# Attention scores: a stage of nine blocks for each head pair from the sixth on, in one tile of four PSUM banks; the last weight pieces fetched behind the first rows of the last stage

## The chip, the cores and the metric

The kernel runs on one core of one Trainium2 chip. The metric is the device time of one execution in microseconds (us); lower is better. [...]

## What is computed

The reference is a windowed causal attention whose output goes through a gated feed-forward network (FFN), all in fp32:

```python
B, H, S, D = 8, 8, 576, 64                     # q, k, v: (B, H, S, D)
scores = q @ k.T / sqrt(D)                     # for each batch and head
rel = pos[:, None] - pos[None, :]
bias = slopes[h] * -abs(rel)
scores = where((rel >= 0) & (rel < 128), scores + bias, -1e9)
attn = softmax(scores) @ v
x = attn.transpose(0, 2, 1, 3).reshape(B * S, H * D)      # 4608 x 512
gate = 1 / (1 + exp(-(x @ w_gate)));  val = x @ w_val     # 512 x 1536
out = (gate * val) @ w_out                                 # 1536 x 512
```

## The kernel before

Work is first put into a graph: every operation is added with an engine, an assumed cost and the keys that it reads and writes. A planner (`Graph.order`) then plays the engines forward and fixes one order of instructions for each engine, which the chip runs in that order; the table `TUNE` shifts the wishes (`want`) of some operations at random and so only changes this order. On the chip each engine runs its own list strictly in order, with semaphores between engines. Transfers are issued by SyncE (SP), accumulating ones by GpSimd (POOL).

**Attention.** A unit is one batch and one pair of heads: 32 units, each with 9 blocks of 128 query rows (the 1152 tokens of two heads). A block's scores come from matmuls on quarter arrays (64 rows by 64 columns; there are four of them, here called lanes, a row half `r` by a column half `h`). A block takes one matmul per column half, each over three 64-key squares (two for the first block of a unit). `scores` (L566) does a *stage*: four blocks until the fifth unit's end (48 blocks in twelve stages), then eight blocks (thirty stages), in banks mm2 to mm5; the blocks run on from unit to unit, so that a stage of eight straddles units. Even blocks go to one row half, odd ones to the other. Then VectorE (DVE) folds each bank in place with a `copy_predicated` (L583, two blocks an instruction), takes scale, bias and row maximum (L591), ScalarE (ACT) takes the exponential and its sum (L595), DVE or ACT normalise (L673, L674), TensorE transposes three blocks at a time (L680), and the weighted sum of values follows: `values` (L718) for the first eight units, `split_values` (L637) from the ninth on. `split_values` has two phases, which stand directly before and directly behind a later stage of scores, all on quarter arrays.

**First FFN pass.** Between stages TensorE works on `ffn` (L808): groups of three 512-column matmuls. It starts as soon as the first weights are decoded and the first four units are through; early on it is short of input.

**Second FFN pass and last stage.** `ffn2` (L998) does the rest of the gated products by a scheme with 7 products per 2 by 2 block; `last` (L1166) does the output projection in three rounds with 15 products each in the sequence 11, 2, 13, 0, 12, 3, 5, 4, 9, 6, 10, 7, 1, 8, 14. Each product reads rows from DRAM (`rows_...`), which are split into a high and a low part (`duo`, L308 and L1147 on ACT, L317 and L1148 on DVE), some after sums and differences (L1086). Its weights were stashed in DRAM and come back by `fetch_o`: the six pieces `wo<-sums_o`, which ACT (L933) and DVE (L934) split after landing, and four pieces `wo_ar0`, `wo_ar5`, `wo_w2s`, `wo_h` (`parts_o`), which need no splitting and are used by the later products only. The meeting of `ffn2` and `last` is called the seam here.

## Time and profile before

| | us |
|---|---|
| median of 3 runs (943.48 to 945.67) | 943.83 |
| the profiled execution, its time | 943.45 |
| the profiled execution, its span | 941.7 |
| TensorE busy in the span | 931.8 (99%) |
| VectorE busy | 788.7 (84%) |
| ScalarE busy | 518.4 (55%) |

The span runs from the first to the last instruction; the time has 1.75 us more, which lie around it. A matmul's end is modelled and matmuls overlap, so a busy TensorE may still wait inside; the chain of work that ended last tells such waits better than the busy time. It is 95% matmuls: L998 45%, L1166 25%, L808 12%, the scores L566 5%, L637 4%, L680 4%.

### The profile page before, as it was taken

The page shows a single profiled execution, that of the slowest core. Times are in us where ns is not written, and L with a number is a line of the kernel's source. Part 1 is how long each engine was busy: PE and PEld are TensorE (multiplying, and loading weights), DVE is VectorE, ACT ScalarE, POOL GpSimd, SP SyncE. Part 2 cuts the span into 40 slices and gives each one's busy share as a digit, 9 for nine tenths or more (in the row PEclk, how much of TensorE's full clock was granted, in tenths as well). Part 3 has the DMA queues.
Part 4 walks back from the last instruction along what each step waited for, and adds up shares of the span by engine and source line. Part 5 has one row for each costly group of instructions (what it writes and reads, how often), then busy time and mean ns, then how long its engine had stood idle before and what let it go on. Part 6 is the DMA issues. An engine that isn't in the chain of part 4 may idle for free.

```text
span 941.7 us, 18317 instructions
## 1 busy us (share of the span) xinstructions
PE 931.8 (99%) x6334; PEld 789.1 (84%) x6334; DVE 788.7 (84%) x1946; ACT 518.4 (55%) x1345; POOL 202.4 (21%) x381
## 2 busy tenths in 40 slices
PE   8999999999999999999999999999999999999998
PEld 6778888888878888888889999988887888888886
DVE  8999888998898996878787697764797899797897
ACT  8998789889874453444344344443563434334341
POOL 3544436545620000112111222211110000000000
PEclk9999999999999999999999999999999999999999
DMA  8887779976937444669878979979897481564441
GB/s 303 282 291 264 234 271 288 345 254 201 330 94 246 145 149 142 146 154 240 234 203 216 295 218 315 249 180 261 251 285 277 156 294 64 167 222 148 121 147 68
DMA packets 91485, 205.94 MB, mean 219 GB/s; under 512 B 9984, under 2 KB 28416, under 8 KB 91008
## 3 DMA queue, kind: packets, MB, share of 16 engines
q1 hardware_dynamic: 79584, 185.56, 57.4%
q0 software_dynamic: 11520, 18.88, 13.4%
q8 instruction: 50, 0.82, 0.3%
q14 instruction: 43, 0.35, 0.1%
q10 hardware_dynamic: 288, 0.33, 0.1%
HBM read 123.73 MB, written 81.00 MB: 217 GB/s over the span
## 4 chain that ended last, share of the span: by engine, by line
PE 95%; ACT 2%; DMA 2%; DVE 1%; issue 0%; SPq 0%; DVEq 0%; ACTq 0%
PE mm L998 45%; PE mm L1166 25%; PE mm L808 12%; PE mm L566 5%; PE mm L637 4%; PE mm L680 4%; DMA rows_ar<-hid 1%; PE mm L718 1%; ACT pb L595 1%; DMA early_ar<-in_q_dram 0%; DVE pb L673 0%; DVE mm L583 0%; ACT kept L595 0%; ACT early_h L308 0%; PE mm L396 0%
## 5 line engine op out<-in xcount | busy, mean ns | idle before, releaser
L998 PE MATMUL mm<-xc,w2s 128*128 128x512 f32 (+1 forms) x2016 | 423.0, 371 | 0.0
L998 PEld LDWEIGHTS mm<-xc,w2s 128*128 128x128 f32 x2016 | 368.7, 188 | 53.3 <-ACT shared L308 0.4
L1166 PE MATMUL mm<-duo,wo 128*128 128x512 f32 x756 | 173.4, 389 | 1.8 <-DVE duo L317 1.8
L1166 PEld LDWEIGHTS mm<-duo,wo 128*128 128x128 f32 x756 | 141.7, 188 | 32.0 <-DVE duo L317 2.6
L808 PE MATMUL mm<-first,first 128*128 128x512 f32 x480 | 130.0, 407 | 0.6 <-ACT early_h L308 0.4
L308 ACT COPY low<-mm 128x512 f32<-128x512 f32 (+1 forms) x93 | 51.3, 553 | 100.6 <-DVE mm L1005 56.4
L808 PEld LDWEIGHTS mm<-first,first 128*128 128x128 f32 x480 | 84.4, 189 | 16.4 <-ACT early_h L308 0.6
L1010 ACT ACTIVATE sg<-mm 128x512 f32<-128x512 f32 (+3 forms) x108 | 54.3, 522 | 71.2 <-PE mm L998 47.6
L1005 DVE TENSOR_TENSOR mm<-mm,low 128x512 f32<-128x512 f32 (+1 forms) x96 | 62.1, 651 | 36.4 <-PE mm L998 34.6
L756 POOL DMA_DIRECT2D hidq<-later_hs x47 | 42.2, 970 | 205.7 <-DVE later_hs L1015 133.8
L595 ACT ACTIVATE pb<-pb,st 128x128 f32<-128x128 f32 x216 | 84.4, 398 | 0.9 <-DVE st L591 0.9
L691 POOL TENSOR_SCALAR_AFFINE_SELECT pt<-early_h 128x384 f32<-128x384 f32 x96 | 53.5, 581 | 39.2 <-ACT early_h L308 34.0
L691 POOL TENSOR_SCALAR_AFFINE_SELECT pt<-spread 128x384 f32<-128x384 f32 x96 | 49.5, 544 | 49.0 <-ACT spread L308 45.0
L583 DVE COPY_PREDICATED mm<-early_h,mm 128x256 f32<-128x256 int32 (+1 forms) x144 | 50.6, 389 | 3.3 <-PE mm L566 2.8
L637 PEld LDWEIGHTS mm<-pt,vr 64*64 64x64 f32 x1056 | 42.8, 133 | 9.8 <-ACT pb L595 2.9
L591 DVE CUSTOM_DVE_ANT_0 pb<-mm,early_h 128x128 f32<-128x128 f32 x216 | 49.8, 283 | 0.0
L637 PE MATMUL mm<-pt,vr 64*64 64x192 f32 (+2 forms) x1056 | 46.7, 284 | 0.0
L756 POOL DMA_DIRECT2D hidq<-shared x25 | 22.3, 990 | 101.1 <-DVE shared L1015 91.9
L308 ACT CAST duo<-rows_xr 128x1024 fp32r<-128x1024 f32 x20 | 21.1, 1054 | 39.8 <-PE mm L1166 33.1
L595 ACT ACTIVATION_READ_ACCUMULATOR pb<-pb,st 128x1 f32 x216 | 42.1, 195 | 0.0
L673 DVE TENSOR_SCALAR pb<-pb,st 128x128 f32<-128x128 f32 x164 | 40.2, 292 | 1.8
L308 ACT COPY early_h<-mm 128x384 f32<-128x384 f32 (+3 forms) x76 | 32.4, 446 | 9.9 <-PE mm L637 7.2
(200 smaller groups left out, 1431.8 us busy)
## 6 DMA issues: line engine op xcount, KB each, us to landing
hid<-later_hs SPq DMA_DIRECT2D x38, 256.0 KB, 4.4
vr<-in_v_dram SPq DMA_DIRECT2D x32, 288.0 KB, 5.7
hidq<-later_hs POOLq DMA_DIRECT2D x36, 256.0 KB, 6.0
wraw<-in_moe_w_gate_dram SPq DMA_DIRECT2D x14, 512.0 KB, 5.8
wraw<-in_moe_w_val_dram SPq DMA_DIRECT2D x14, 512.0 KB, 4.4
kr<-in_k_dram SPq DMA_DIRECT2D x11, 576.0 KB, 5.2
wraw<-in_moe_w_out_dram SPq DMA_DIRECT2D x12, 512.0 KB, 7.4
early_h<-in_k_dram SPq DMA_DIRECT2D x10, 576.0 KB, 5.0
```

The source lines that it names most:

```text
L308: g.add("ACT", act_cost(n, psum), lambda: nc.scalar.copy(out(), src()), reads, writes, want, release=release, slack=slack, gives=gives, wa ...
L583: g.add("DVE", dve_cost((a1 - a0) * P, psum=True), lambda b=b, a0=a0, a1=a1: nc.vector.copy_predicated(quads(b)[:, a0:a1, 1:3], before[:, ...
L591: g.add("DVE", 0.21, lambda: nc.vector.tensor_tensor_reduce(pb()[:, e], sp[b][:, a, D:D + P], relm[u.p][:, w], op0=ALU.add, op1=ALU.min, s ...
L595: g.add("ACT", 0.39, lambda: nc.scalar.activation(pb()[:, e], pb()[:, e], AF.Exp, bias=st()[:, e:e + 1], scale=-1.0, accum_out=st()[:, 3 + ...
L637: nc.tensor.matmul(mm[both[h].at][e * D:(e + 1) * D, a - e * S - cuts[h]:b - e * S - cuts[h]], vraw(u)[r * D:r * D + D, c], seen, start=fi ...
L691: nc.gpsimd.affine_select(pt(u)[:, f0:f0 + 2 * n - 1:2, :], both(), [[0, n], step], cmp, 0.0, base=0, channel_multiplier=mult)
L756: g.add("POOL", 1.2, lambda to=to, of=of: nc.gpsimd.dma_start(to(), of(), accum_op=ALU.add), keys, parts_, F, size=2 * kb / 300.0, port=False)
L808: nc.tensor.matmul(mm[s.at][:, 0:wd], w.tile(kind, wi, i)[:, c * P:(c + 1) * P], xpart(x, c)[:, 0:wd], start=(k == 0 and c == 0), stop=(k ...
L998: nc.tensor.matmul(mm[b][:, 0:N2], w.tile2(i, wp)[:, wk, c * P:(c + 1) * P], combo(k, xp, N2)[:, c], start=(start and c == 0 and j == 0), ...
L1005: g.add("DVE", dve_cost(N2, psum=True), lambda: nc.vector.tensor_tensor(o(), bk(b)(), a(), op=ALU.add), [("mm", b), *reads] if okeys else ...
L1010: g.add("ACT", act_cost(y - x, psum=True), lambda x=x, y=y, s=s: nc.scalar.activation(sg[h]()[:, x:y], bk(b)()[:, x:y], AF.Tanh, scale=0.5 ...
L1166: nc.tensor.matmul(mm[b], wo2(z, part_)[:, i, j * P:(j + 1) * P], duo(xp)[:, m], start=start and q == 0 and m == 0 and e == 0, stop=q == 1 ...
```

## The change

From the sixth unit on (`SOON = 5`) a stage is one unit: nine blocks, one `scores` call for each, 27 stages. The five units before it keep stages of four, the last of them five: eleven stages in place of twelve. The nine blocks lie in one tile of four banks (`area`) that is allocated in place of the banks mm2 to mm5 and given back before the second FFN pass (`four_banks`). In it a block begins three squares behind the one before, so that the two column halves of neighbouring blocks share the squares; blocks 0 to 3 and two thirds of block 4 use one row half and banks 0 and 1, the others the other row half and banks 2 and 3. A matmul that would cross a bank is cut in two: 22 matmuls a unit in place of 18. Keys are laid out accordingly, and a unit's key load has 12 of 18 squares (384 KB in place of 576 KB). The fold is four `copy_predicated` a unit, on 64 partitions each and over three or four blocks, all of them ahead of the first maximum. `split_values` of a unit goes around the scores two units later. In `last` the four `parts_o` transfers of the first round depend, in the planner, on the last sum into the rows called "01". The table `TUNE` is another.

```diff
-RUN = 8
-VLATE = RUN
+RUN = 4
 SOON = 5
+MID = NBLK // 2
+KEY1 = 2 * MID - 2
+KEYS = TOK // D - KEY1
...
-    mm = [ps_m.tile([P, NB], F32, name=f"mm{i}") for i in range(8)]
+    mm = [ps_m.tile([P, NB], F32, name=f"mm{i}") for i in range(2)]
+    mm += [None] * 4 + [ps_m.tile([P, NB], F32, name=f"mm{i}") for i in (6, 7)]
+    four = [ExitStack(), None]
+
+    def four_banks(name):
+        four[0].close()
+        four[0] = ctx.enter_context(ExitStack())
+        pool = four[0].enter_context(tc.tile_pool(name=f"ps_{name}", bufs=1, space=PSUM))
+        if name == "area":
+            four[1] = pool.tile([P, 4 * NB], F32, name=name)
+            nc.vector.memset(squares()[0:D, 3], 0.0)
+            nc.vector.memset(squares()[D:P, 3 * MID + 2], 0.0)
+        else:
+            mm[2:6] = [pool.tile([P, NB], F32, name=f"{name}{i}") for i in range(2, 6)]
...
+    def places(i):
+
+        got = []
+        for h in range(2):
+            a, key, step, n = (3 * i + 2, 2 * i, -1, 3) if h == 0 else (3 * i + 1, 2 * i - 1, 1, 3)
+            if (i, h) in ((0, 0), (MID, 1)):
+                a, key, n = 3 * i + 2 + h, 2 * i + h, 1
+            elif (i, h) == (0, 1):
+                a, key, n = a + 1, key + 1, 2
+            elif (i, h) == (MID + 1, 0):
+                n = 2
+            while n:
+                m = min(n, 8 - a % 8)
+                got.append((a // 16, h, a, key, step, m))
+                a, key, n = a + m, key + step * m, n - m
+        return got
+
+    def scores(u, pend=None):
...
+        todo = sorted(x for lane in lanes.values() for x in lane)
+
+        def matmuls():
+            for _, r, h, i, a, key, step, n in todo:
+                rows, k = slice(r * D, r * D + D), key - r * KEY1
+                last = k + step * n
+                keys = kraw(u)[rows, k:(last if last >= 0 else None):step]
+                nc.tensor.matmul(squares()[h * D:(h + 1) * D, a:a + n], qraw(u)[rows, i - r * MID, h * D:(h + 1) * D], keys, start=True, stop=True)
...
+        def fold(h, k0, k1):
+            n, rows, own, off = k1 - k0, slice(h * D, (h + 1) * D), 2 + h, 4 if h == 0 else 1
+            at = lambda x: squares()[rows, 3 * k0 + x:3 * (k1 - 1) + x + 1:3]
+            g.add("DVE", dve_cost(n * D, psum=True), lambda: nc.vector.copy_predicated(
+                at(own), before[rows, 0:1, h].to_broadcast([D, n, D]), at(off)), ["before"],
...
+        for h, k0, k1 in ((0, 1, MID + 1), (1, 1, MID), (0, MID + 2, NBLK), (1, MID + 1, NBLK)):
+            fold(h, k0, k1)
...
-    def fetch_o(z):
-        F, keys = FIRST + 1.5, [("stash_o", z, i) for i in range(14)]
+    def fetch_o(z, after=()):
+        F, keys = FIRST + 1.5, [("stash_o", z, i) for i in range(14)] + list(after)
...
-        for z in range(len(SLOTS), len(SLOTS) + len(LATER)) if t == 0 else ():
-            fetch_o(z)
+        if t == 0:
+            g.add("PY", 0.0, lambda: None, [("row", *rows["01"][1])], ["first rows"], F)
+            for z in range(len(SLOTS), len(SLOTS) + len(LATER)):
+                fetch_o(z, ["first rows"])
```

Three places of the order follow. The first is TensorE at one stage of scores that stands between the two phases of `split_values`. Before, a stage of eight blocks, its sixteen matmuls in banks mm_73 and mm_75, then mm_74 and mm_76, the last phase behind it (mm_72 and mm_77 are the banks of the values):

```order
L566 MATMUL mm_73<-kr_193,qr_200 64x192
L566 MATMUL mm_75<-kr_193,qr_200 64x192
...
L566 MATMUL mm_75<-early_h_181,early_xr 64x128
L566 MATMUL mm_73<-kr_193,qr_200 64x192
L566 MATMUL mm_75<-early_h_181,early_xr 64x128
L566 MATMUL mm_74<-early_h_181,early_xr 64x192
L566 MATMUL mm_76<-early_h_181,early_xr 64x192
...
L637 MATMUL mm_77<-pt_484,vr_242 64x192 x2
L637 MATMUL mm_72<-pt_484,vr_242 64x192 x2
```

Now, the middle and the end of a stage of nine blocks (L646 is the scores' line of the changed kernel, L705 that of the values):

```order
L646 MATMUL area<-early_h_184,early_xr 64x192 x4
L646 MATMUL area<-early_h_184,early_xr 64x64
L646 MATMUL area<-early_h_184,early_xr 64x128
L646 MATMUL area<-early_h_184,early_xr 64x64
L646 MATMUL area<-early_h_184,early_xr 64x128
L646 MATMUL area<-early_h_184,early_xr 64x192
L646 MATMUL area<-early_h_184,early_xr 64x128
L646 MATMUL area<-early_h_184,early_xr 64x192
L646 MATMUL area<-early_h_184,early_xr 64x64
L646 MATMUL area<-early_h_184,early_xr 64x192 x2
L705 MATMUL mm_73<-pt_303,vr_213 64x192 x2
```

A stage now holds one unit and has short matmuls of one and two squares between the long ones; the phases of the values around it are what they were.

The second place is SP's queue at the seam. Before (rows_hs_7410 and the first rows_ar are the two halves of the rows called "12", wo_7390 is the sixth piece of the first six weights):

```order
L313 DMA rows_hs_7348<-hid_128 128x1024
L313 DMA wo_7390<-sums_o_116 128x1792
L313 DMA hid_123<-shared 128x512
L313 DMA wo_ar_7406<-parts_o_120 128x2048
L313 DMA rows_hs_7410<-hid_139 128x1024
L313 DMA wo_ar_7426<-parts_o_119 128x2048
L313 DMA hid_129<-shared 128x512
L313 DMA rows_ar_7456<-hid_140 128x1024
L313 DMA rows_ar_7456<-hidq_169 128x1024
L313 DMA wo_w2s_7469<-parts_o_117 128x3584
```

Now (rows_hs_7495 stands for rows_hs_7410, wo_7500 for wo_7390):

```order
L309 DMA rows_hs_7434<-hid_131 128x1024
L309 DMA hid_126<-shared 128x512
L309 DMA rows_hs_7495<-hid_142 128x1024
L309 DMA wo_7500<-sums_o_119 128x1792
L309 DMA hid_132<-shared 128x512
L309 DMA hid_139<-later_hs_7259 128x512
L309 DMA rows_ar_7570<-hid_143 128x1024
L309 DMA rows_ar_7570<-hidq_172 128x1024
L309 DMA wo_w2s_7668<-parts_o_120 128x3584
L309 DMA wo_h_7671<-parts_o_121 128x1536
L309 DMA rows_wraw_6758<-hidq_173 128x1024
L309 DMA wo_ar_7681<-parts_o_122 128x2048
```

Both wo_ar have moved behind the rows, and the sixth piece wo_7500 has moved from ahead of the rows_hs load to behind it.

The third place is VectorE at the seam. Before (duo_7285 and duo_7381 are the two halves of product 13's rows, then of product 12's):

```order
L934 TENSOR_TENSOR wo_7390<-wo_7390,wo_7461 128x1792
L317 TENSOR_TENSOR duo_7285<-rows_xr,duo_7285 128x1024
L1086 TENSOR_TENSOR rows_tt<-rows_tt,rows_hs_7410 128x1024
L317 TENSOR_TENSOR duo_7381<-rows_xr,duo_7381 128x1024
L1086 TENSOR_TENSOR rows_xr<-rows_tt,rows_xr 128x1024
L317 TENSOR_TENSOR duo_7444<-rows_hs_7348,duo_7444 128x1024
L1086 TENSOR_TENSOR rows_xr<-rows_xr 128x1024
L1086 TENSOR_TENSOR rows_hs_7348<-rows_hs_7348,rows_ar_7456 128x1024
L1086 TENSOR_TENSOR rows_xr<-rows_hs_7348,rows_xr 128x1024
L317 TENSOR_TENSOR duo_7285<-rows_wraw_6619,duo_7285 128x1024
```

Now (duo_7485 and duo_7542 are these halves):

```order
L313 TENSOR_TENSOR duo_7485<-rows_xr,duo_7485 128x1024
L1002 TENSOR_TENSOR wo_7500<-wo_7500,wo_7595 128x1792
L313 TENSOR_TENSOR duo_7542<-rows_xr,duo_7542 128x1024
L313 TENSOR_TENSOR duo_7523<-rows_tt,duo_7523 128x1024
L1154 TENSOR_TENSOR rows_tt<-rows_tt,rows_hs_7495 128x1024
L313 TENSOR_TENSOR duo_7531<-rows_hs_7434,duo_7531 128x1024
L1154 TENSOR_TENSOR rows_xr<-rows_tt,rows_xr 128x1024
L1154 TENSOR_TENSOR rows_hs_7434<-rows_hs_7434,rows_ar_7570 128x1024
L313 TENSOR_TENSOR duo_7485<-rows_wraw_6758,duo_7485 128x1024
```

The splits that product 13 needs no longer stand behind a row sum, but the second of them stands directly behind the split of the sixth weight piece. In both kernels the sum that waits for rows_ar stands ahead of the split for product 12.

## Rows read from the trace of the kernel before

**Rows 1.** The page, busy us (share of the span) xinstructions

```profile
PE 931.8 (99%) x6334; PEld 789.1 (84%) x6334; DVE 788.7 (84%) x1946; ACT 518.4 (55%) x1345; POOL 202.4 (21%) x381
```

**Rows 2.** Busy time by stretch: PE, PEld, DVE, ACT, POOL, clock, DMA share, GB/s

```profile
20.00:40.00 20.00, 19.06 (x238) 14.28 (x238) 19.81 (x104) 18.93 (x76) 10.08 (x25) 1.00 0.77 253
60.00:80.00 20.00, 20.00 (x211) 16.11 (x210) 19.63 (x95) 17.77 (x67) 9.52 (x23) 1.00 0.81 274
```

**Rows 3.** The chain that ended last, 118 to 133 us: start, length, what

```profile
120.08 0.85 PE mm L637 x18
...
120.99 1.30 PE mm L566 x30
122.29 0.66 PE mm L637 x20
...
124.12 0.65 PE mm L680 x6
124.78 3.45 PE mm L808 x15
```

**Rows 4.** The same chain over the whole span

```profile
21.80 1.45 PE mm L566 x30
...
84.09 0.85 PE mm L637 x18
...
142.84 1.46 PE mm L566 x31
...
272.83 413.94 PE mm L998 x1980
...
693.58 3.87 PE mm L1166 x17
```

**Rows 5.** VectorE's groups by form: count | busy us, mean ns | idle before

```profile
L591 DVE CUSTOM_DVE_ANT_0 pb<-mm,early_h 128x128 f32<-128x128 f32 x216 | 49.8, 283 | 0.0
...
L583 DVE COPY_PREDICATED mm<-early_h,mm 128x256 f32<-128x256 int32 x112 | 43.8, 419 | 3.3 <-PE mm L566 2.8
L673 DVE TENSOR_SCALAR pb<-pb,st 128x128 f32<-128x128 f32 x164 | 40.2, 292 | 1.8
...
L591 DVE DVE_READ_ACCUMULATOR2_ANT st<- 128x1 f32 x288 | 23.4, 81 | 0.0
...
L317 DVE TENSOR_TENSOR first<-early_xr,first 128x512 fp32r<-128x512 f32 x16 | 10.3, 682 | 0.0
...
L583 DVE COPY_PREDICATED mm<-early_h,mm 128x128 f32<-128x128 int32 x32 | 9.1, 285 | 0.0
```

**Rows 6.** Timeline of TensorE at the seam: start, length, idle before in brackets

```profile
703.71 7.09 PE L1166 MATMUL mm<-duo,wo 128*128 128x512 f32 x30 [0.16 <-DVE duo L317]
712.43 3.94 PE L1166 MATMUL mm<-duo,wo 128*128 128x512 f32 x16 [1.63 <-DVE duo L317]
```

**Rows 7.** Timeline of SP's queue at the seam

```profile
685.22 0.32 SPq L313 DMA_DIRECT2D wo<-sums_o  x1
...
695.71 0.32 SPq L313 DMA_DIRECT2D rows_hs<-hid  x1
696.08 1.42 SPq L313 DMA_DIRECT2D wo_ar<-parts_o  x1
```

**Rows 8.** Timeline of VectorE at the seam

```profile
696.36 2.03 DVE L934 TENSOR_TENSOR wo<-wo,wo 128x1792 fp32r<-128x1792 f32 x1 [0.22 <-ACT wo L933]
...
711.16 2.35 DVE L317 TENSOR_TENSOR duo<-rows_wraw,duo 128x1024 fp32r<-128x1024 f32 x2
```

**Rows 9.** ScalarE's groups, 680 to 712 us

```profile
L933 ACT CAST wo<-wo 128x1792 fp32r<-128x1792 f32 x3 | 5.2, 1718 | 0.0
```

**Rows 10.** Landing of wo (560 to 700); accumulating transfers, 300 to 400 and 660 to 690

```profile
DMA to landing us min/median/max: 5.0/7.0/7.9
...
hidq<-later_hs POOLq DMA_DIRECT2D x3, 256.0 KB, 4.0
...
hidq<-later_hs POOLq DMA_DIRECT2D x6, 256.0 KB, 8.9
```

More of the change, by code (lines that the diff above doesn't have):

```diff
@@ L573, in scores @@
         writes, release = [("mm", 2 + b) for b in used], max(u.rel(i) for u, i in blks)
-        then = split_values(pend, want, reads, writes, release) if pend else lambda: None
-        g.add("PE", cost, matmuls, reads, writes, want, slack=0.0 if pend else slack, release=release, mode=1)
-        then()
-        while put_off:
-            probabilities(*put_off.pop(0))
+        g.add("PE", cost, matmuls, reads, writes, want, release=release, mode=1)
         for b, on in sorted(used.items(), key=lambda kv: blks.index(kv[1][0][:2])):
@@ new lines, in early_scores @@
+            if i == VDELAY * TRI - 1 and 0 < u.n <= VHEAD:
+                done(units[u.n - 1])
+    def places(i):
[13 more added lines that the diff above has]
+        return got
@@ new lines, in scores @@
+    def scores(u, pend=None):
+        want = u.when(0)
+        slack = 0.0 if u.n < HEAD else SLACK
+        lanes = {}
+        for i in range(NBLK):
+            for r, h, a, key, step, n in places(i):
+                lane = lanes.setdefault((r, h), [])
+                at = lane[-1][0] + lane[-1][-1] if lane else 0
+                lane.append((at, r, h, i, a, key, step, n))
+        todo = sorted(x for lane in lanes.values() for x in lane)
[5 more added lines that the diff above has]
+                nc.tensor.matmul(squares()[h * D:(h + 1) * D, a:a + n], qraw(u)[rows, i - r * MID, h * D:(h + 1) * D], keys, start=True, stop=True)
+        cost = max(lane[-1][0] + lane[-1][-1] for lane in lanes.values()) * D / 600.0 - 0.05
+        reads = [(x, u.l, i) for x in ("qr", "kr") for i in range(NBLK)]
+        writes, release = [("mm", 2 + b) for b in range(4)], u.rel(NBLK - 1)
+        then = split_values(pend, want, reads, writes, release) if pend else lambda: None
+        g.add("PE", cost, matmuls, reads, writes, want, slack=0.0 if pend else slack, release=release, mode=1)
+        then()
+        while put_off:
+            probabilities(*put_off.pop(0))
+        def fold(h, k0, k1):
[3 more added lines that the diff above has]
+                at(own), before[rows, 0:1, h].to_broadcast([D, n, D]), at(off)), ["before"],
+                  [("mm", 2 + b) for b in sorted({(3 * k + x) // 8 for k in range(k0, k1) for x in (own, off)})], want)
+        for h, k0, k1 in ((0, 1, MID + 1), (1, 1, MID), (0, MID + 2, NBLK), (1, MID + 1, NBLK)):
+            fold(h, k0, k1)
+        for i in range(NBLK):
+            exps(u, i, lambda i=i: four[1][:, (3 * i + 2) * D:(3 * i + 4) * D], sorted({(3 * i + 2) // 8, (3 * i + 3) // 8}))
+            if i % TRI == TRI - 1:
+                if u.n >= VHEAD:
@@ L1221, in attention_gated_ffn @@
     stages = [0]
-    stream = [(u, i) for u in units for i in range(NBLK)]
+    stream = [(u, i) for u in units[0:SOON] for i in range(NBLK)]
     load(units[0], True, False)
@@ L1236, in attention_gated_ffn @@
         while at < min(len(stream), (u.n + 1) * NBLK + VDELAY * TRI):
[L1237 to L1244 removed]
+            n = len(stream) - at if len(stream) - at <= RUN + 1 else RUN
+            early_scores(stream[at:at + n])
+            at += n
+        if u.n == SOON:
+            g.add("PY", 0.0, lambda: four_banks("area"), [], [("mm", 2 + b) for b in range(4)], u.when(0))
+        if u.n >= SOON:
+            scores(u, pend.pop(0) if pend and pend[0].n <= u.n - 2 else None)
+        if u.n >= VHEAD:
+            pend.append(u)
+            if u.n + NSLOT < len(units):
+                load(units[u.n + NSLOT], True, False)
         if u.n == 0:
@@ L1289, in attention_gated_ffn @@
     g.add("PY", 0.0, lambda: None, [], ["lent"] + [("mm", z) for z in POOL], FIRST)
+    g.add("PY", 0.0, lambda: four_banks("later"), [], [("mm", 2 + b) for b in range(4)], FIRST)
     head = list(zip(range(KEEP2), stay))
```

88 lines of the change are left out of this document (44 added, 44 removed), and 7 rows, old and new, of the table TUNE.

## The prediction

> **What bounds the kernel now.** I read the page first, then busy time by stretch, then the chain that ended last, and only then single timelines. The page says that TensorE is busy 99% of the span [rows 1], so what counts is what it executes, and where it waits behind that figure. The stretches tell two parts apart. From 20 to 80 us VectorE is busy 19.81 and 19.63 of each 20 us [rows 2]: up to here it is VectorE (with ScalarE close behind) that sets the pace, and TensorE is short of work. Then the chain becomes one unbroken row of matmuls: the first phase of the values of the ninth unit at 84.09, and from 272.83 on 413.94 us of second-pass matmuls without a piece of anything else [rows 4]. A microsecond of matmuls that disappears between 84 and 272 us is therefore a microsecond of the end, unless a wait appears. The third part is the seam, where TensorE waits 0.16 and 1.63 us for VectorE's split of rows [rows 6].
>
> **What a stage costs.** A stage of eight blocks between the phases of the values takes 1.30 us to the start of the next phase [rows 3]; a stage that stands alone takes 1.46 [rows 4], since it pays for entering and leaving the quarter arrays itself. In a full stage of eight each lane has four matmuls over three squares, twelve squares of 64 keys: 1.30 / 12 = 0.108 us a square. Check: in the second phase of the values the longest lane has 192 + 128 + 64 = 384 columns, six squares, and takes 0.66 us [rows 3], 0.110 a square. So time goes by the columns of the longest lane. In a stage of nine, written out from `places`, all four lanes have exactly twelve squares (five or six matmuls each). I take the same price: 1.30 inside, 1.46 alone. A unit's nine blocks now cost what eight did.
>
> The trace does not show a stage with 22 matmuls. The other bound is that time goes by matmul. Each is executed as two passes, each with its weight load: 32 passes in 1.30 us are 41 ns each, 20 in 0.66 us are 33 ns [rows 3]. Now there are 44. At 33 ns the stage takes 1.45, at 41 ns 1.79. I take 1.30, because the values' phase, of which more than half is shorter than three squares, keeps the price by square and not the price by pass. Below 1.30 nothing can go while a lane has twelve squares.
>
> [...]
>
> **From 84 us to the seam.** Both programs have the same 22 stages inside values phases behind the first such phase. What differs there, counted in the two orders: before, 384 matmuls of the first FFN pass, 201 transposes and two lone stages; now 402, 204 and none. The FFN matmuls cost 3.45 / 15 = 0.230 us each [rows 3]: 18 x 0.230 = +4.1. Three transposes cost half of 0.65 [rows 3]: +0.3. The two lone stages, of which one is shown: -2 x 1.46 = -2.9 [rows 4]. Sum +1.5 us: less of the FFN has been done when the first values phase comes.
>
> **Up to 84 us.** Work ahead of that first phase, again counted: TensorE does 18 fewer FFN matmuls (-4.1), three fewer transposes (-0.3), and its stages change from twelve of four blocks and six of eight to ten of four, one of five and five of nine. Two stages of four in a row take 1.45 [rows 4]; with 0.73 for four, 0.95 for five (estimated from 0.108 a square) and 1.46 for eight or nine, 17.5 becomes 15.6, -1.9. All together -6.3. But VectorE is the one that is full. By the last maximum ahead of the first values phase it does 90 blocks in place of 96: 6 x (0.283 + 0.081) = -2.2; the folds go from 37 of 256 columns and 11 of 128 to 17 and 6, plus ten of 256 and ten of 192, whose duration I put at 0.35 between the two shown (bounds 0.285 and 0.419), so -8.4 - 1.4 + 4.2 + 3.5 = -2.1; five fewer normalisations, -5 x 0.292 = -1.5 [rows 5]; two fewer subtractions of 512 columns, -1.4 [rows 5], for one more cast, estimated at two thirds of one, +0.5. Sum -6.7, from which the overlap comes off: two splits of 1.22 take 2.35 together [rows 8], 0.09 a joint, with 22 joints 2.0. So -4.7 for VectorE, against -6.3 for TensorE; VectorE being the slower to gain, I go by it, and with the two fills below it is -4.5. What can eat it: all four folds now stand ahead of the first maximum and wait for the whole stage, about 1.5 us of folds where one of 0.419 stood. VectorE has weights to decode meanwhile, which is the cover; without it five stages could hold it by a microsecond each. Bounds: 0 to -6.3.
>
> The smaller key loads (384 KB for 576) lie behind other work and nothing on the chain waits for them; nothing. The handing over of the four banks costs two small fills on VectorE, 0.2 us, taken off above.
>
> **The seam.** Before, VectorE stands at the sum that needs rows_ar, and product 12's split waits behind it. Now rows_ar no longer has two megabytes of weights ahead of or beside it, and is needed later than it lands. But the sixth weight piece has got behind the rows_hs load, which SP could issue only at 695.71, while the piece left at 685.22 before [rows 7]. Queued behind it: it would leave where wo_ar did, at 696.08; such a piece takes 5.0 to 7.9 us to land [rows 10], then 1.72 on ScalarE [rows 9], 2.03 on VectorE [rows 8], and directly behind stands product 13's second split, 1.2. So the split is ready at 706.0 to 708.9. TensorE, counted in the order, has 48 matmuls from the end of the second pass (693.58, [rows 4]) until it needs that split; at 0.227 that is 10.9 us, 704.5. That would be a stall of 1.5 to 4.4. Against it: what rows_hs waits for are accumulating transfers, which land in 8.9 us in the crowd before the seam and in 4.0 in a quiet stretch [rows 10], and 1.9 MB of weights have left that crowd. I take 2.5 us earlier and a middle landing of 7.0: stall 1.0 in place of 1.79 [rows 6], -0.8; bounds +2.6 and -1.8.
>
> **Sum.** -4.5 + 1.5 - 0.8 = -3.8. On the profiled execution's 943.45 this is 939.65; the median of the runs lies 0.38 above that execution, so I predict 940.0 us.
>
> **Rivals.** (1) *The gain up to 84 us is mostly held up*: VectorE waits at the folds for whole stages. For it: nine warming matmuls more stand in TensorE's list than before (28 for 19), put where the planner expects holes. Against it: VectorE had almost no idle time to lose work to, and it keeps the same decoding. If 3 of the 4.5 go, -0.8: 943. (2) *The sixth weight piece becomes the wait at the seam*: nothing lands earlier, a stall of 3 to 4.4. It gives -4.5 + 1.5 + 1.2 to 2.6, so 942 to 943.5. (3) *Slower: passes, not columns, set the stage.* 27 stages at 1.45 add 4.0 us, total +0.2; at 1.79 they add 13.2, total +9.4, 953. It decides from about 35 ns a pass on (44 x 35 = 1.54; 27 x 0.24 = 6.6 more, which is slower by 0.3%). The 33 ns of the values' phase stand just under it, but there they are explained by the columns. (4) *TensorE alone sets the early part*: -6.3 + 1.5 - 0.8, so 938.2; for it speaks that matmuls already fill 19.06 to 20.00 of each 20 us there [rows 2], against it that these include waits.
>
> **Numbers.** A measurement of this kernel tells about 0.3% (2.8 us) from no change: the bounds are 941.0 and 946.7. Forecast 0.45 (938.5 to 941.5), rival 4 0.13, rival 1 0.22, rival 2 0.11, rival 3 0.09. Faster: rival 4, most of the forecast (0.39) and the lower edge of rivals 1 and 2 (0.04): 0.56. Slower: nearly all of rival 3, 0.08. Same: 0.36. The range 936.5 to 944.5 leaves out rival 3 and the tails of the others. The forecast's own range is 938.5 to 941.5.
>
> **What would show it.** Right: stages inside the values phases of 1.30 to 1.33 us and lone ones of 1.46 to 1.50; the first values phase near 79.5 (84.09 - 4.5); the long run of second-pass matmuls ending about 3 us earlier than 693.58; at the seam one stall of about 1 us, at product 13 and not at product 12. Wrong: stages of 1.45 or more; pieces of VectorE at the folds on the chain between 40 and 80 us; the sixth weight piece's split on the chain with more than 2 us; or a pause of TensorE between 80 and 690 us, where I have assumed none because there was none before.

## The result: 1.35% slower

The changed kernel takes 957.2 us (median of 4 runs, 956.68 to 957.71), the kernel before 944.4 beside it: ratio 1.0135, 95% interval 1.0117 to 1.0152. The prediction, 940.0 with a range of 936.5 to 944.5, was wrong, in sign too. The profiled execution has a span of 956.0 us.

The page of the changed kernel, busy us and share of the span by engine:

```profile
PE 936.7 (98%) x6568; PEld 790.4 (83%) x6568; DVE 802.5 (84%) x1941; ACT 524.4 (55%) x1338; POOL 203.3 (21%) x382
```

VectorE has 13.8 us more than before, though five instructions fewer [rows 1]. By stretch (start:end, length, then busy us of PE, PEld, DVE, ACT, POOL, granted clock, DMA share, GB/s), two of 20 us, and the whole attention up to the long run of second-pass matmuls:

```profile
40.00:60.00 20.00, 16.76 (x235) 13.51 (x237) 18.73 (x79) 17.14 (x63) 11.36 (x24) 1.00 0.75 236
...
220.00:240.00 20.00, 18.80 (x239) 15.21 (x237) 18.59 (x91) 13.66 (x56) 8.59 (x20) 1.00 0.57 182
...
0.00:287.18 287.18, 271.60 (x3478) 220.06 (x3479) 260.05 (x1191) 233.89 (x889) 139.78 (x309) 1.00 0.74 237
```

The last of these, for the kernel before, ends at 272.67:

```profile
0.00:272.67 272.67, 268.18 (x3256) 221.36 (x3257) 245.19 (x1190) 236.12 (x906) 135.29 (x306) 1.00 0.81 269
```

The attention ends 14.5 us later, and VectorE was busy 14.9 us longer in it. That pair of numbers is the thread of what follows.

TensorE's timeline: the first values phase, the end of the attention, and the seam.

```profile
87.06 0.63 PE L748 MATMUL mm<-ident,pb 128*128 128x128 f32 x3 [0.40 <-DVE pb L741]
87.62 0.92 PE L705 MATMUL mm<-pt,vr 64*64 64x192 f32 x22
...
287.18 4.37 PE L1066 MATMUL later<-xc,w2s 128*128 128x512 f32 x18
...
705.95 1.52 PE L1234 MATMUL later<-duo,wo 128*128 128x512 f32 x6
707.30 1.52 PE L1066 MATMUL mm<-xc,w2s 128*128 128x512 f32 x6
708.66 6.96 PE L1234 MATMUL later<-duo,wo 128*128 128x512 f32 x30
715.47 2.88 PE L1234 MATMUL mm<-duo,wo 128*128 128x512 f32 x12
```

The first values phase comes at 87.62, not at 79.5 (before 84.09, [rows 4]). From there to the second pass it is 199.6 us, where before it was 188.7. At the seam the two pauses of [rows 6] are gone. The chain of work that ended last was one row of matmuls from 84 us on before. Now it can be followed back to 223.31 us only, and between there and the second pass it has other engines in it:

```profile
226.03 1.40 DVE w2s L313
...
227.89 1.17 DVE pb L741 x2
...
231.99 1.54 ACT pb L557 x8
233.53 1.16 ACT early_h L557 x6
...
250.55 1.31 PE area L646 x26
...
258.70 1.31 PE area L646 x26
```

The stage itself costs what was forecast: 1.31 us inside the values phases, 0.01 from the 1.30 of a stage of eight [rows 3].

Where VectorE's time comes from stands in its timeline. Before, a stage's four folds and its first maximum:

```profile
121.70 1.42 DVE L583 COPY_PREDICATED mm<-early_h,mm 128x256 f32<-128x256 int32 x4
123.03 0.28 DVE L591 CUSTOM_DVE_ANT_0 pb<-mm,early_h 128x128 f32<-128x128 f32 x1
```

In the changed kernel, three normalisations at 50 us and three at 123, then the folds and first maxima of a unit:

```profile
50.15 0.94 DVE L741 TENSOR_SCALAR early_h<-early_h,st 128x128 f32<-128x128 f32 x3
...
122.90 0.68 DVE L741 TENSOR_SCALAR kept<-kept,st 128x128 f32<-128x128 f32 x3
124.28 1.22 DVE L659 COPY_PREDICATED area<-early_h,area 64x256 f32<-64x256 int32 x3 [0.70 <-PE area L646]
125.53 0.29 DVE L553 CUSTOM_DVE_ANT_0 pb<-area,early_h 128x128 f32<-128x128 f32 x1
125.75 0.08 DVE L553 DVE_READ_ACCUMULATOR2_ANT st<- 128x1 f32 x1
125.86 0.44 DVE L659 COPY_PREDICATED area<-early_h,area 64x256 f32<-64x256 int32 x1
126.34 0.29 DVE L553 CUSTOM_DVE_ANT_0 pb<-area,early_h 128x128 f32<-128x128 f32 x1
```

Add start and length. Before, the folds end at 123.12 and the maximum starts at 123.03, 0.09 ahead of that end. Now they end at 125.50 and the maximum starts at 125.53; the next fold and the next maximum also start 0.03 to 0.04 behind. In the single records of the trace 164 joints beside a fold are without overlap, 153 of them 0.03 us behind like these; before there are 9. Such a joint costs 0.12 us: 0.09 of overlap that is gone and 0.03 behind. The lines also set right what "The change" says of the folds: only in 7 of the 27 units do all four folds stand ahead of the first maximum; in 16 the fourth comes directly behind it, as here, and in 4 others one or two folds come later still. Counted from the point where the instruction ahead could have been overlapped to the start of the one behind, the folds take VectorE about 60 us, before 44.5, although their durations sum to less (51.7 and 56.0).

Two things can cause it, and the program shows both. The folds work on partitions 0 to 63 and 64 to 127 in turn. And all of them write one tile, so that the program lets each wait for VectorE's own preceding instruction, whatever bank that touched; so it stands in VectorE's list (DVE_49 is VectorE's own semaphore):

```
L659 COPY_PREDICATED area_696<-early_h3_93,area_696 64x3x64 [waits DVE_49] x2
L553 ISA pb3_300,st6_388<-area_696,early_h3_93 128x128 [waits DVE_49]
L553 ISA st6_388 128x1
L659 COPY_PREDICATED area_696<-early_h3_93,area_696 64x4x64 [waits DVE_49]
```

### The profile page after: what moved, and what is told of

It is laid out like the page before. It is cut to its first block, busy times and chain, and to the rows that moved or that the text cites. A ratio compares the mean times of both kernels' runs of the same rounds, so it can differ in the third digit from the quotient of the medians.

```text
span 956.0 us, 18836 instructions
## 1 busy us (share of the span) xinstructions
PE 936.7 (98%) x6568; PEld 790.4 (83%) x6568; DVE 802.5 (84%) x1941; ACT 524.4 (55%) x1338; POOL 203.3 (21%) x382
## 4 chain that ended last, share of the span: by engine, by line
PE 74%; DVE 1%; ACT 1%; issue 0%; POOL 0%; DVEq 0%
PE later L1066 22%; PE mm L1066 22%; PE later L1234 15%; PE mm L1234 10%; PE mm L876 2%; PE mm L705 1%; PE mm L748 1%; PE area L646 1%; ACT pb L557 0%; DVE pb L741 0%; DVE pb L553 0%; DVE area L659 0%; DVE w2s L313 0%; DVE xc L313 0%; ACT early_h L557 0%
## 5 line engine op out<-in xcount | busy, mean ns | idle before, releaser
L1066 PE MATMUL later<-xc,w2s 128*128 128x512 f32 (+1 forms) x1008 | 224.3, 371 | 0.4 <-DVE st L738 0.4
L1066 PE MATMUL mm<-xc,w2s 128*128 128x512 f32 (+1 forms) x1008 | 223.9, 371 | 0.0
L1066 PEld LDWEIGHTS later<-xc,w2s 128*128 128x128 f32 x1008 | 184.6, 188 | 26.8 <-PE mm L748 0.6
L1066 PEld LDWEIGHTS mm<-xc,w2s 128*128 128x128 f32 x1008 | 184.8, 188 | 26.3
L1234 PE MATMUL later<-duo,wo 128*128 128x512 f32 x432 | 100.7, 389 | 0.0
L1234 PEld LDWEIGHTS later<-duo,wo 128*128 128x128 f32 x432 | 81.1, 188 | 16.8
L1234 PE MATMUL mm<-duo,wo 128*128 128x512 f32 x324 | 75.7, 389 | 0.0
L1234 PEld LDWEIGHTS mm<-duo,wo 128*128 128x128 f32 x324 | 60.8, 188 | 12.6
L1073 DVE TENSOR_TENSOR later<-later,low 128x512 f32<-128x512 f32 (+1 forms) x48 | 31.3, 651 | 25.0 <-PE later L1066 24.8
L705 PEld LDWEIGHTS mm<-pt,vr 64*64 64x64 f32 x1056 | 40.7, 133 | 12.0 <-issue 3.4
L659 DVE COPY_PREDICATED area<-early_h,area 64x256 f32<-64x256 int32 (+1 forms) x108 | 42.8, 397 | 6.0 <-PE area L646 2.7
L705 PE MATMUL mm<-pt,vr 64*64 64x192 f32 (+2 forms) x1056 | 46.4, 286 | 1.1 <-DVE turn L714 0.6
```

The lines of the kernel that those rows point to most:

```text
L659: g.add("DVE", dve_cost(n * D, psum=True), lambda: nc.vector.copy_predicated(at(own), before[rows, 0:1, h].to_broadcast([D, n, D]), at(off ...
L705: nc.tensor.matmul(mm[both[h].at][e * D:(e + 1) * D, a - e * S - cuts[h]:b - e * S - cuts[h]], vraw(u)[r * D:r * D + D, c], seen, start=fi ...
L1066: nc.tensor.matmul(mm[b][:, 0:N2], w.tile2(i, wp)[:, wk, c * P:(c + 1) * P], combo(k, xp, N2)[:, c], start=(start and c == 0 and j == 0), ...
L1073: g.add("DVE", dve_cost(N2, psum=True), lambda: nc.vector.tensor_tensor(o(), bk(b)(), a(), op=ALU.add), [("mm", b), *reads] if okeys else ...
L1234: nc.tensor.matmul(mm[b], wo2(z, part_)[:, i, j * P:(j + 1) * P], duo(xp)[:, m], start=start and q == 0 and m == 0 and e == 0, stop=q == 1 ...
```

## The experiments

Unless said otherwise, every engine's list of instructions is that of the kernel it is made from, and only the instructions named differ. "Before" is 943.5 to 944.6 us throughout; each ratio is to its runs beside the same kernel.

**Form of the folds.** `a_whole` folds two blocks an instruction on all 128 partitions, in the same tile:

```diff
-            nc.vector.copy_predicated(at(own), before[rows, 0:1, h].to_broadcast([D, n, D]), at(off))
+            nc.vector.copy_predicated(own2(k), before, off2(k))          # k = 1, 3, 5, 7; 128 x (2 blocks x 2 squares)
```

> The changed kernel with the order of every engine kept; only the form of the four folds of a unit is another: 128 partitions, two blocks, the plain mask, as before the change (0.42 us each; 1024 columns a unit in place of 896). Theory 1, the switch of partitions: in the changed kernel a fold on partitions 0 to 63 or 64 to 127 begins 31 to 34 ns behind the end of the instruction ahead of it, where the folds of before began 84 ns ahead of that end, since VectorE does not overlap instructions that begin at another partition; a unit's folds then take VectorE 0.116 + 0.422 + 0.032 + 0.373 + 0.034 + 0.354 + 0.034 + 0.440 + 0.034 = 1.84 us, and 4.5 folds of before 4.5 x 0.337 less the half-full ones = 1.36. In whole form 4 x 0.337 = 1.35, so 27 x 0.49 = 13 us come back: 943 to 947 us, and the folds begin 84 ns early again. Theory 2, the one tile: each fold waits for VectorE's own previous one, because all four lie in one tile; these waits stay, so the joints stay near +34 ns and the time is 956 to 959. Theory 3, the order (the table of numbers) is at fault: the order is the same, so 956 to 959.

952.25 us (ratio to before 1.0089, 1.0074 to 1.0104): 5.0 us back (4.3 by the ratios), between the theories. VectorE's timeline and busy time:

```profile
122.62 1.36 DVE L668 COPY_PREDICATED area<-early_h,area 128x256 f32<-128x256 int32 x3 [0.73 <-PE area L648]
124.02 0.29 DVE L555 CUSTOM_DVE_ANT_0 pb<-area,early_h 128x128 f32<-128x128 f32 x1
```

```profile
0.00:281.69 281.69, 269.08 (x3478) 220.36 (x3479) 256.30 (x1193) 233.84 (x889) 139.44 (x309) 1.00 0.75 242
```

The first fold of a unit now starts 81 ns ahead of the end before it, but a fold or a maximum directly behind a fold still starts 34 ns behind (123.98 and 124.02): the own waits stay.

**Two regroupings.** `a_grouped` issues lower, lower, upper, upper; `a_two` issues one fold of eight blocks on either half.

```diff
-        for h, k0, k1 in ((0, 1, MID + 1), (1, 1, MID), (0, MID + 2, NBLK), (1, MID + 1, NBLK)):
+        a_grouped: ((0, 1, MID + 1), (0, MID + 2, NBLK)) in the first fold's place, ((1, 1, MID), (1, MID + 1, NBLK)) in the second's
+        a_two:     (0, 1, NBLK) in the first fold's place, (1, 1, NBLK) in the second's
```

> The changed kernel with the order of every engine kept, the four folds of a unit in the sequence lower half, lower half, upper half, upper half in place of lower, upper, lower, upper. Theory 1 (switch of partitions): three joints a unit without overlap in place of five, 2 x 0.117 x 27 = 6.3 us less of VectorE's time: 950 to 953 us; the second fold of each pair begins early. Theory 2 (own waits in one tile): the waits are as many as before: 956 to 959. Theory 3 (order): 956 to 959.

961.5 us (1.0188, 1.0173 to 1.0203): slower. Every fold on half the partitions directly behind another, also on the same half, still starts 34 to 35 ns behind it (64 of 64), so theory 1 alone is refuted. Why it is slower than the changed kernel is not shown: all four folds now stand together and the joints without overlap are fewer (139 for 164), yet VectorE is busy 1.4 us longer (the normalisations alone take 1.2 us more) and idle 2.4 us longer.

```profile
0.00:290.96 290.96, 273.27 (x3479) 219.70 (x3479) 261.42 (x1191) 232.55 (x889) 141.00 (x309) 1.00 0.73 234
```

> The changed kernel with the order kept, two folds a unit in place of four: one of eight blocks (64 x 512) on each half of the partitions, 1024 columns a unit in place of 896. From 0.354 to 0.373 us for 192 columns and 0.422 to 0.440 for 256, 67 ns for 64 more, a fold of 512 takes about 0.69. Theory 1: three joints without overlap, 0.116 + 0.69 + 0.032 + 0.69 + 0.034 = 1.56 us a unit in place of 1.84, 27 x 0.28 = 7.5 us less: 948 to 952. Theory 2: one own wait in place of three, and 2 x 0.155 us of fixed cost less, about 1.5 a unit: also 947 to 951. Theory 3: 956 to 959.

955.0 us (1.0119, 1.0104 to 1.0134), 2.2 less: the joints of the second and third fold went, the columns grew (1024 a unit for 896).

**The price put into the kernel before.** `b_halves` splits one fold of each stage of eight (30 of them) into a lower and an upper half.

```diff
+                    for h, own, off in ((0, 1, 3), (1, 2, 0)) if not b and at >= SOON * NBLK else ():
+                        rows = slice(h * D, (h + 1) * D)
+                        nc.vector.copy_predicated(quads(b)[rows, a0:a1, own], before[rows, a0:a1, h], quads(b)[rows, a0:a1, off])
```

> The kernel before with its order kept, but the fold of the first of the four banks of each stage of eight (30 folds) made as two, one on the lower and one on the upper 64 partitions, over 128 columns each. Theory 1 (switch of partitions): 0.29 + 0.034 + 0.29 + 0.034 = 0.64 us in place of 0.337, 30 x 0.305 = 9 us more for VectorE, which is busy 88% of the stretch from 84 to 273 us, so that half to all of it shows: 948 to 953 us. Theory 2 (one tile): the two halves lie in a tile of their own bank as before and the cost is one more instruction, 30 x 0.07 = 2 us for VectorE, nearly all hidden: 943.5 to 945.5. Theory 3 (order): no change, 943.5 to 945.5.

950.2 us (1.0069, 1.0052 to 1.0085). The lower half's joint to the upper half (34 to 35 ns behind, all 30) carries an own wait too, since the halves share a tile; the instruction behind the upper half has none, and 27 of 30 still start 30 to 33 ns behind. VectorE's busy time rises by 10.9 us, and the attention ends 5.8 us later. Ahead of the first values phase 2.2 us more work make it 2.8 us later. Behind it, 8.7 us more make the stretch 3.0 us longer: most of it went into VectorE's idle time there. The three rows are the whole attention and the stretch behind the first values phase, then that stretch before:

```profile
0.00:278.48 278.48, 271.36 (x3257) 220.75 (x3258) 256.11 (x1220) 236.34 (x905) 136.04 (x306) 1.00 0.80 263
86.79:278.48 191.69, 190.54 (x2429) 159.03 (x2429) 174.89 (x820) 161.88 (x631) 97.24 (x212) 1.00 0.79 255
...
84.09:272.80 188.71, 188.71 (x2429) 159.62 (x2429) 166.14 (x796) 161.02 (x628) 96.49 (x211) 1.00 0.80 261
```

**One tile in the kernel before.** `b_onetile` makes mm2 to mm5 slices of one tile for the whole attention, `b_onetile_late` only from the sixth unit on, as in the change.

```diff
+    area = pool.tile([P, 4 * NB], F32, name="area")
+    mm[2:6] = [area[:, i * NB:(i + 1) * NB] for i in range(4)]
```

> The kernel before with every engine's order kept; only the four banks of the scores are slices of one tile until the second pass, as in the changed kernel, in place of four tiles. Theory 2 (one tile: a fold or a maximum waits for the instruction of VectorE directly before it, though that one touched another bank): the folds that follow one another begin 31 to 35 ns behind instead of 84 to 91 ns ahead, 0.12 us each; with three to five such joints in each of 30 stages that is 11 to 18 us more for VectorE, of which in the run with halved folds 6.75 of 11.5 us came through: 950 to 957 us. Theory 1 (the switch of partitions alone): no partition is switched, 943 to 945. Theory 3 (order alone): 943 to 945.

961.2 us (1.0168, 1.0148 to 1.0187). Of the 16.6 us, 14.6 lie ahead of the first values phase (98.64 for 84.02), where stages of four share the tile and TensorE waits 7.6 us for VectorE to be done with it; the changed kernel doesn't have that. Hence:

> The kernel before with its order kept; the four banks are one tile only for the stages of eight, from the sixth unit on, where the changed kernel has it too (two small fills are added, 1.1 us of VectorE). Of the 16.6 us that one tile for the whole attention cost, 14.6 stood ahead of the first values phase, where stages of four share it. Theory A: what stays is the own waits of the folds, 3.4 us behind the first values phase as measured there and 1 to 4 us in the six stages ahead of it: 947 to 952. If one tile costs only where stages of four share it: 944 to 945.5.

951.9 us (1.0077, 1.0059 to 1.0095), 7.3 more for the tile and its handing over; but for two added fills no instruction of the attention is changed or moved. Not all of it is own waits: at the handing over TensorE stands 2.21 us for the second fill, and in this profiled execution, the longest of the four (953.65 us), the granted clock was 0.83 from 40 to 50 us. Behind the first values phase, where the one tile is all that differs, the stretch is 192.5 us for 188.7: 3.9 us for the tile, against 3.4 expected. The wait at the handing over, then the four folds of a stage:

```profile
42.74 2.20 PE L590 MATMUL area<-early_h,early_xr 64*64 64x192 f32 x24 [2.21 <-DVE area L334]
...
121.65 1.68 DVE L607 COPY_PREDICATED area<-early_h,area 128x256 f32<-128x256 int32 x4 [0.41 <-PE area L590]
123.36 0.29 DVE L615 CUSTOM_DVE_ANT_0 pb<-area,early_h 128x128 f32<-128x128 f32 x1
```

From first fold to first maximum it is 1.71 us (one of the four covers a single block), before 1.33 with four full ones.

**The order.** Three kernels without the table: `TUNE = ()`.

> The kernel before with an empty TUNE. Theory 3 (what was lost is the fit of the order): the table of before is worth most of the 13 us, so about 950 to 957 us here, as slow as the changed kernel. Theories 1 and 2: the table may be worth something, but the changed kernel without its table is still 10 us or more behind this one.

> The changed kernel with an empty TUNE. Theory 3: as slow as before without its table, within 3 us. Theories 1 and 2: 10 us or more behind before without its table.

> The changed kernel with an empty TUNE and whole folds (128 partitions). Theories 1 and 2: 3 to 7 us faster than the changed kernel without its table, as with the table (5.0). Theory 3: the form of the folds matters little in an order that was not fitted to it; the two agree within 2 us.

947.6 us (1.0030, 1.0019 to 1.0040), 974.2 and 969.8. The table of before is worth 3.0 us, that of the changed kernel 17; without tables the changed kernel is 26.6 behind and not level, so theory 3 falls. Whole folds save 4.4 here, as they do with the table. How much of the 17 is the clock's is not shown: in the profiled execution of `a_notune` TensorE was idle 23.7 us of the attention (15.6 in the changed kernel with its table) and the granted clock was 0.96 there (0.986 over its span).

```profile
0.00:306.06 306.06, 282.36 (x3486) 229.93 (x3486) 266.21 (x1200) 237.80 (x898) 139.24 (x309) 0.96 0.70 228
```

**Both causes removed.** `a_twotiles` gives banks 0, 1 and banks 2, 3 a tile each, folds in whole form (block 4, whose squares lie in both tiles, by a small fold of its own), and alternates the tiles:

```diff
-        for h, k0, k1 in ((0, 1, MID + 1), (1, 1, MID), (0, MID + 2, NBLK), (1, MID + 1, NBLK)):
-            fold(h, k0, k1)
+        row = [whole(1, 2), whole(5, 2), whole(3, 1), whole(7, 2), middle]      # tiles 0, 1, 0, 1, 0 from 1
+        # then maxima 0 1 2 3 5, middle, maxima 6 4 7 8
```

> The changed kernel with the order of all engines kept apart from VectorE's folds and maxima within a unit: whole folds (128 partitions), and the four banks as two tiles of two banks, the folds alternating between the tiles, so that an access waits for no instruction directly before it. Theory A (the folds' lost overlap, by the switch of partitions and by the own waits of one tile, is the cause): the joints without overlap fall from 164 to under 40, the folds' time on VectorE from 60.0 us to about 45, and since 0.6 to 1 of such time has come through so far (6.75 of 11.5, 5.0 of 3.1), 9 to 15 us come back: 942 to 948, with 190 to 193 us from the first values phase to the second pass (199.6 now, 194.4 with whole folds alone). Theory B (the stage of nine itself: all nine maxima must be read before the next stage may write, and the exponentials come in bunches): no more than with whole folds alone, 950 to 953.

945.9 us. Two of its 288 maxima stood behind their exponentials, which so took old values; `a_twotiles2` has them ahead:

> The changed kernel with two tiles of two banks and whole folds, as in the run a_twotiles, and with every maximum ahead of its exponential (there two of the 288 stood behind). Theory A: the same time as that run, 944 to 948 us, and 190 to 192 us from the first values phase to the second pass; with before at 943.5 to 944.6 the loss of 13 us is gone but for 1 to 3. Theory B: if those two had saved a wait, up to 1 us more.

946.4 us (1.0023, 1.0014 to 1.0033): 10.8 of the 13 us are back. The folds start up to 92 ns ahead again (14 joints are left of 164), and VectorE's busy time falls by 12.5, the attention's end by 11.8:

```profile
126.83 1.29 DVE L679 COPY_PREDICATED area<-early_h,area 128x256 f32<-128x256 int32 x4 [0.71 <-PE area L663]
128.03 0.29 DVE L558 CUSTOM_DVE_ANT_0 pb<-area,early_h 128x128 f32<-128x128 f32 x1
```

```profile
0.00:275.42 275.42, 266.98 (x3478) 219.96 (x3478) 247.54 (x1220) 232.72 (x889) 142.08 (x309) 1.00 0.78 248
```

The fourth corner, two tiles with folds on halves (lower of either tile, upper of either tile):

> The fourth corner of form and tile: two tiles of two banks, but the folds on half the partitions as in the changed kernel (lower half of either tile, then upper half of either tile). Changed kernel 957.2, whole folds alone 952.25, whole folds and two tiles 945.9. If the two causes add (the switch of partitions 5.0, the own waits 6.4): own waits gone, 957.2 - 6.4 = 951; and the joints behind and ahead of an upper half stay at 31 to 35 ns, those between two lower halves go to -84. If the switch of partitions is the stronger in the absence of own waits, so that the joints stay: 953 to 957. If own waits are all that counts: 946 to 948.

952.4 us (1.0082, 1.0063 to 1.0101). One cause removed gives 5.0 (form) or 4.8 (tile), both give 10.8 (by the ratios 4.3, 5.0 and 10.6): they add, nearly. The joint between two upper halves is at -95 ns, that from lower to upper at +31, the one behind an upper half at +31 to 32.

**Total time or the first maximum?** In the runs so far the time also went with how late a stage's first maximum began. `a_early` puts maxima 0 to 2 ahead of the last two folds of the changed kernel, `a_twotiles3` does so in `a_twotiles2`.

```diff
-        folds 1 2 3, maximum 0, fold 4, maxima 1 2 3 ...                    # changed kernel, most units
-        folds 1 2 3 4, maxima 0 1 2 3 5 ...                                 # a_twotiles2
+        a_early:      folds 1 2, maxima 0 1 2, folds 3 4, maxima 3 ...
+        a_twotiles3:  folds 1 2, maxima 0 1 2, folds 4 3, maximum 5, middle, maxima 6 3 4 7 8
```

> The changed kernel (folds on half the partitions, one tile) with the order kept, but within a unit the maxima of blocks 0 to 2 stand ahead of the folds of banks 2 and 3 instead of behind them. VectorE's work is the same, with one joint without overlap more. Theory C (what counts is how late the first maximum of a stage begins, since exponentials, sums, normalising and transposes hang on it): counted from the stage's first matmul it begins 4.54 us later in the changed kernel, 4.99 with grouped folds (961.5 us), 4.63 with two folds (955.0), 4.28 with whole folds (952.25), 4.30 with two tiles and halves (952.4), 3.94 with both (946.4); here about 3.9, so 946 to 951 us. Theory D (only VectorE's total time counts): 27 x 0.12 us more of it, 957 to 960.

> The kernel a_twotiles2 (two tiles, whole folds, no joint without overlap) with the maxima of blocks 0 to 2 behind the second of the five folds instead of the fourth. Theory C: the first maximum begins about 0.5 us earlier (3.94 now), so up to 27 x 0.5 x 0.67 = 9 us, as far as TensorE had waited for it: 940 to 944, which would be at or under before. Theory D: VectorE's time is the same, 945.5 to 947.

959.8 us (1.0168, 1.0154 to 1.0182) and 945.9 (1.0018, 1.0009 to 1.0027). The first maximum began 0.54 and 0.62 us earlier, and nothing clear of noise was gained: theory C falls, and both times lie where theory D put them. The row below, of `a_early`, has a granted clock of 0.99, so a part of its 2.6 us may be the clock's.

```profile
0.00:288.75 288.75, 271.92 (x3478) 221.18 (x3478) 261.51 (x1191) 234.11 (x889) 136.55 (x309) 0.99 0.74 236
```

**The seam by itself.** `b_seam_held` is the kernel before with the two wo_ar issued behind the rows of product 12:

```diff
-        move(lambda: as32(wo2(z)), lambda: stash_o[z], ...)                  # both wo_ar, ahead of and between the rows "12"
+        (the same two, issued after the second half of the rows "12")
```

> The kernel before with every engine's order kept, but the two transfers wo_ar of the first round issued behind the rows of product 12 instead of ahead of and between them (the part of the change that concerns the seam, by itself). Theory A: the pause of 1.79 us at the seam goes, as in the changed kernel, and nothing else moves: 1.4 to 1.9 us faster than before. If the pause comes from VectorE's queue and not from those transfers: no change, within 0.4 us.

943.1 us, ratio 0.9980 (0.9968 to 0.9991), 1.5 us less where 1.4 to 1.9 were expected if those transfers make the pause: the pause is gone, TensorE's row at the seam has no break, and this kernel is ahead of both. In its profiled execution the attention, whose instructions are the same as before, ends 1.3 us later than in that of before (273.99 for 272.67); so far apart can two single traces lie.

```profile
695.09 30.10 PE L1182 MATMUL mm<-duo,wo 128*128 128x512 f32 x132
```

**All of them in one view.** VectorE's busy time up to the second pass, the start of that pass, and the difference:

| kernel | us | VectorE busy | second pass at | difference |
|---|---|---|---|---|
| before | 944 | 245.2 | 272.7 | 27.5 |
| b_seam_held | 943.1 | 245.4 | 274.0 | 28.6 |
| b_notune | 947.6 | 250.3 | 278.1 | 27.8 |
| b_halves | 950.2 | 256.1 | 278.5 | 22.4 |
| b_onetile_late | 951.9 | 256.5 | 282.2 | 25.7 |
| b_onetile | 961.2 | 258.2 | 290.7 | 32.5 |
| a_twotiles | 945.9 | 246.7 | 274.9 | 28.3 |
| a_twotiles3 | 945.9 | 246.5 | 274.7 | 28.3 |
| a_twotiles2 | 946.4 | 247.5 | 275.4 | 27.9 |
| a_tiles_half | 952.4 | 254.0 | 281.5 | 27.5 |
| a_whole | 952.25 | 256.3 | 281.7 | 25.4 |
| a_two | 955.0 | 254.9 | 283.7 | 28.8 |
| changed kernel | 957.2 | 260.1 | 287.2 | 27.1 |
| a_early | 959.8 | 261.5 | 288.8 | 27.2 |
| a_grouped | 961.5 | 261.4 | 291.0 | 29.5 |
| a_whole_notune | 969.8 | 262.8 | 299.9 | 37.1 |
| a_notune | 974.2 | 266.2 | 306.1 | 39.8 |

Leave out `b_onetile` and the two changed kernels without a table. Then busy time varies by 16 us and the idle time beside it by 7, so the end of the attention mostly follows what VectorE must do there. This is read from the table and is no fixed rule: `b_halves` and `b_onetile_late` filled 5.1 and 1.8 us of the idle time, and the three left out have 5 to 12 us more of it than the kernel before, where TensorE waited and, in two of them, the clock fell (over the span 0.986 in `a_notune` and 0.993 in `a_whole_notune`).

## Why the prediction failed, step by step

**What bounds the kernel: wrong, and the root of it.** "A microsecond of matmuls that disappears between 84 and 272 us is therefore a microsecond of the end" was read from the unbroken chain of [rows 4], and so VectorE's work behind 84 us was costed at nothing. In the kernel before TensorE's row was unbroken and VectorE nearly full beside it: it idled 22.6 us of those 188.7, which had room for a part of more work only. There b_halves gave it 8.7 us more and the stretch grew by 3.0; the changed kernel gave it 14.1 us more and the stretch grew by 10.9. The assumption "no pause of TensorE between 80 and 690, because there was none before" fell with it.

**Up to 84 us: wrong (-4.5 forecast, +3.6 measured).** The failed term is the folds: "-2.1", from durations of 0.35 and 0.285 to 0.419 and an overlap of 0.09 at each joint. The durations were near (0.363 and 0.431 measured); the overlap, taken for granted, was not there at most joints. Counted with their joints the folds ahead of the first values phase went from 14.8 to 17.2 us. The second term is the normalisations, "-1.5" for five fewer: from start to next start they took 16.3 us instead of 13.7. Eleven lasted more than 0.32 us, before one, such as those at 50.15 above, 0.94 for three; each of them ran while GpSimd was at work, ten times at a select:

```profile
50.30 0.52 POOL L759 TENSOR_SCALAR_AFFINE_SELECT pt<-spread 128x384 f32<-128x384 f32 x1
```

All ten that began with 0.29 us or more of a select still to run are among the eleven, and each of them ended 0.07 to 0.08 us behind that select; of the 31 that ran with GpSimd idle none took more than 0.29. That a running select makes a normalisation longer is read from these records and was not tried. In a_twotiles2 the folds are back at 14 us, the normalisations are not (15.5), and the first values phase is at 83.99: still no gain ahead of it, with VectorE busy 1.3 us less there and idle 1.2 us more. The handing over of the four banks, put at 0.2 us, is a part: in the changed kernel TensorE stands 1.06 us until 40.74, just behind the second fill (40.53 to 40.64), and VectorE then 0.50 us. The rest of these 4.5 us stays without an experiment.

**From 84 us to the end of the attention: the counts right, the sum wrong.** Counted work was to add 1.5 us; measured from the first values phase to the end, without the seam's 1.8, it is +12.5 in the changed kernel and +4.4 in a_twotiles2. The 8.1 between come from the folds' form, tiles and sequence together; 2.9 remain unexplained.

**The stage: right.** 1.31 us inside the phases, and lone ones 1.47 to 1.48 from the first matmul to the next of another kind. This is what the columns of the longest lane give (twelve squares at 0.108, 1.30) and not what the 44 passes do (1.45 to 1.79), so rival 3 did not happen, though the time that it gave for its dearer case (953) was the nearest of all.

**The seam: the old pause rightly gone, the new stall wrong.** Forecast -0.8 with a stall of 1.0 left; no stall is left, so the bound of -1.8 came true. Two terms for the sixth piece were off, in opposite directions. It was issued 8.1 us ahead of the end of the second pass (700.69, for 708.83 by the chain), where the forecast had it leave as that pass ends. And it landed in 9.6 us, longer than the whole range of 5.0 to 7.9. Product 13's second split ended at 717.81, half a microsecond before TensorE came to it at about 718.3, so a stall was missed by that much only. b_seam_held has the removed pause alone at 0.8 to 3.0 us.

```profile
700.69 0.43 SPq L309 DMA_DIRECT2D wo<-sums_o  x1
...
714.66 2.02 DVE L1002 TENSOR_TENSOR wo<-wo,wo 128x1792 fp32r<-128x1792 f32 x1
716.59 1.22 DVE L313 TENSOR_TENSOR duo<-rows_xr,duo 128x1024 fp32r<-128x1024 f32 x1
```

**Rivals.** Rival 1 named the place (the folds ahead of the first maximum) with the wrong mechanism: not waiting for the stage, but dearer folds; its price, 3 of the 4.5 us, is far from the 17 by which the forecast missed. Its premise, all four folds ahead of the first maximum, held in 7 of 27 units.

## What to carry to other kernels

Price an instruction by the time from its start to the next one's start, in the neighbourhood that it will have, not by its duration: here a cut to half the partitions and one tile for four left the folds' durations near what was forecast and cost 10.8 of the 13 us. Work on separate tiles in turn, and keep neighbours on the same partitions: here the one alone gave back 4.8 us, the other 5.0. TensorE's unbroken chain did not make VectorE's idle time free (in b_halves 8.7 us more work lengthened the stretch by 3.0); put added work there and see how much of it moves the end (b_halves took 30 more small instructions) before costing it at nothing.

## What the runs showed of the hardware

Beside a fold, two instructions of VectorE overlapped in the kernel before at 218 of 227 joints, by 71 to 95 ns, mostly 80 to 93. A fold or maximum that waits for the instruction directly ahead started 34 to 35 ns behind its end (the changed kernel, a_whole, b_onetile_late). In b_halves the instruction behind an upper half begins at another partition than that half and has no wait on VectorE itself; in 27 of 30 cases it started 30 to 33 ns behind. The first fold of a unit in the changed kernel looks odd: a lower half behind instructions that begin at partition 0, it still started 30 to 32 ns behind in 21 of 27 units (the other six came 135 to 697 ns behind). The last fold ahead of it was the upper one of the unit before. In a_tiles_half, where a lower fold is a unit's last, the same fold mostly started 75 to 99 ns early. So in these two kernels the joint went with the half of the last fold and not with the instruction directly ahead; why is not shown. Each wait for the instruction directly ahead cost 0.12 us here, and the waits cost 3.9 us in all behind the first values phase of b_onetile_late.
